# An attention-then-MLP kernel: loads of q and k, loads of v, turns and weight transposes put in another order, GpSimd's copies of v put later

## The chip, the cores and the metric

The kernel runs on one core of a Trainium2 chip. Its engines are TensorE (PE in the rows, its weight loads PEld), VectorE (DVE), ScalarE (ACT), GpSimd (POOL) and SyncE (SP). POOL and SP also issue DMAs, and each carries out its instructions in program order: an instruction that waits holds up everything behind it on the same engine. The metric is the device time of one execution in microseconds, lower is better.

## The reference

Two steps follow each other. The first is sliding-window causal attention over 8 batches, 8 heads, 576 rows, head size 64 and a window of 64:

```python
scores = scale * np.matmul(q, k.transpose(0, 1, 3, 2))
mask = (rel >= 0) & (rel < window)          # rel = row - column, window = 64
scores = np.where(mask, scores, -1e9)
attn = exp(scores - max); attn = attn / attn.sum()
x = attn @ v                                # heads side by side: x is 4608 x 512
```

The second is an MLP on the 4608 rows of x, with w_in 512 x 2048 and w_out 2048 x 512:

```python
h = x @ w_in
g = h * np.cos(h)
return g @ w_out
```

## The kernel before

The MLP is cut into nine **stages** `mt` of 512 rows (`MT`), called stage 0 to stage 8 here. A stage has two halves. In the first, 64 matmuls at L359 make h in 16 pieces `ff`; for each piece ScalarE takes the sine (L504), and VectorE multiplies (L507) and so frees the PSUM bank; five banks go round, so TensorE stops when VectorE stops. In the second half 64 matmuls at L519 multiply by w_out. Between two stages stand the 64 small matmuls of `values` (L338), which make the next stage's x from v and the attention weights; VectorE and ScalarE copy the result to `xT`.

The attention of the batches runs beside it. Batch b belongs to stage b-1: in that stage's second half TensorE makes the scores (L263), VectorE adds the mask (L286), ScalarE takes exp (L297), VectorE the reciprocal of the sum (L304), POOL multiplies to the weights `w` (L311, one instruction for a group of three or four blocks), and SP issues the DMA transpose of each group (`wT`, L323). A batch has ten such groups or so in two cuts (`CUTS`): those of the first cut are needed by the `values` at the end of the same stage, those of the second only a stage later.

What a batch needs before that comes in four steps:

- `load_chunk` (L146) loads q and k in five pieces each, with a cast from float32 to bf16; POOL issues them. `load_v` (L152) does the same for v, in five pieces.
- `turn` (L213) is a DMA transpose, issued by SP, from `q` to `qX` and from `k` to `kX`.
- `spread_q` (L221) is four VectorE copies from `qX` into `qB`, the form that the scores read.
- `spread_v` (L156) is two copies inside the tile of v which fill the rows that the `values` of odd blocks read; POOL makes them (L112, `v<-v`), or a DMA from SP (L160).

The order is a plan: `at(time, fn, ...)` puts a step at a planned time, in units where a stage is T = 32 and its second half begins at Q = 16, and `pump(time)` emits all steps that are due, between the matmuls. So the planned time sets where a step stands among the instructions of its engine, and nothing else; t0 = 32(b-1) is the start of batch b's stage. Before the change k and q of batch b are loaded in turns from t0 - T + 5.6, turned at the end of the stage before (t0 - 5.5), and spread at t0 + 6.2; v is loaded at t0 + 0.5 and spread at t0 + 14.45. Batch 2 has planned times of its own. A DMA of POOL also waits until the eighth DMA before it on POOL has landed, since eight semaphores go round.

Of the kernel before, what the change touches and what calls it, by code (L numbers as in the profile page):

```python
# [24 lines left out]
NC = 5  # L25
# [15 lines left out]
T = 2 * Q  # L41
# [17 lines left out]
def kernel(  # L59
# [326 lines left out]
    def at(time, fn, *args):  # L386
        plan.append((time, len(plan), fn, args))
# [25 lines left out]
    for b in range(1, B):  # L413
        t0 = T * (b - 1)
        if b == 1:
            for p in range(PAIRS):
                for lag, fn in ((0, tr_q), (0.01, tr_k), (0.02, put_q), (0.03, put_k)):
                    at(7 + 1.8 * p + lag, fn, b, p)
        else:
            for i, name in enumerate(("k", "q")):  # L420
                for c in range(NC):
                    at((4 + 0.5 * c + 2.5 * i if b == 2 else t0 - T + 5.6 + 1.8 * c + 0.9 * i), load_chunk, name, b, c)
                for c, (lo, hi) in enumerate(((0, 2), (2, 4), (4, 5))):
                    at(t0 - 5.5 + 1.8 * i + 0.6 * c, turn, name, b, lo, hi)
            for c, (lo, hi) in enumerate(((0, 4), (4, 5))):
                for h in range(2):
                    at(t0 + 6.2 + h + 2 * c, spread_q, b, h, lo, hi)
            for c in range(5):
                at(t0 + 0.5 + c, load_v, b, c)
            for half in range(2):  # L430
                at(t0 + (14.45 + 0.1 * half if b > 2 else 10), spread_v, b, half, "p" if b > 2 else "dma")
    for half in range(2):
        at(17.5, spread_v, 1, half, "dma")
    for p in range(PAIRS):
# [32 lines left out]
    turn, turn_h = iter(range(100)), iter(range(100))  # L467
# [17 lines left out]
    for mt in range(n_mt):  # L485
# [23 lines left out]
        half = n_ff // 2 if mt == 0 else n_ff  # L509
# [49 lines left out]
```

## Time and profile before

| | us |
|---|---|
| median of three runs (lowest, highest) | 363.88 (362.71, 371.75) |
| the profiled execution's own time | 364.2 |
| its span, first to last instruction | 362.4 |
| TensorE matmul busy | 304.8 (84%) |
| ScalarE busy | 235.9 (65%) |
| VectorE busy | 227.7 (63%) |
| GpSimd busy | 194.0 (54%) |
| mean granted TensorE clock | 0.939 |

The profiled execution took 364.2 us, 0.3 us over the median, of which 1.8 us lie outside the span. Stages begin, by their first matmul at L359, at 69.12 (stage 1), 100.73, 141.87, 184.19, 225.06, 265.90 and 302.79 us (stage 7). The share of busy time says little here, since the stages have waits in one place and none elsewhere; the rows further down are therefore cut by half stages.

### The profile page before, as it was taken

The page shows a single profiled execution, that of the slowest core. Times are in us where ns is not written, and L with a number is a line of the kernel's source. Part 1 is how long each engine was busy: PE and PEld are TensorE (multiplying, and loading weights), DVE is VectorE, ACT ScalarE, POOL GpSimd, SP SyncE. Part 2 cuts the span into 40 slices and gives each one's busy share as a digit, 9 for nine tenths or more (in the row PEclk, how much of TensorE's full clock was granted, in tenths as well). Part 3 has the DMA queues.
Part 4 walks back from the last instruction along what each step waited for, and adds up shares of the span by engine and source line. Part 5 has one row for each costly group of instructions (what it writes and reads, how often), then busy time and mean ns, then how long its engine had stood idle before and what let it go on. Part 6 is the DMA issues. An engine that isn't in the chain of part 4 may idle for free.

```text
span 362.4 us, 7495 instructions
## 1 busy us (share of the span) xinstructions
PE 304.8 (84%) x2413; PEld 152.9 (42%) x2452; DVE 227.7 (63%) x847; ACT 235.9 (65%) x785; POOL 194.0 (54%) x216
## 2 busy tenths in 40 slices
PE   4769959999993899919995599919996999999996
PEld 2544424444451355404552255404552455454443
DVE  5878836688671875539762786528764876832831
ACT  4887867768982499606983299707984699611720
POOL 9992375798698256870687446970673063000000
PEclk9999978999998699958999699988999899999999
DMA  7999992699999936999399947999399145212002
GB/s 97 180 210 208 178 165 32 116 161 246 114 131 166 189 39 108 128 197 105 81 114 144 218 50 95 149 177 128 75 117 204 49 71 90 90 40 78 1 31 87
DMA packets 166824, 44.02 MB, mean 121 GB/s; under 512 B 155520, under 2 KB 162304, under 8 KB 166784
## 3 DMA queue, kind: packets, MB, share of 16 engines
q0 software_dynamic: 99632, 18.36, 65.0%
q1 hardware_dynamic: 67008, 24.98, 37.4%
q8 instruction: 19, 0.31, 0.4%
q14 instruction: 21, 0.17, 0.2%
q10 hardware_dynamic: 144, 0.20, 0.2%
HBM read 36.70 MB, written 9.44 MB: 127 GB/s over the span
## 4 chain that ended last, share of the span: by engine, by line
PE 32%; DMA 27%; POOL 18%; issue 15%; DVE 5%; ACT 2%; SPq 0%; POOLq 0%; DVEq 0%
PE out_ps L519 17%; DMA qX<-q 14%; POOL w L311 10%; PE h_ps L359 10%; DMA v<-in_v_dram 5%; DMA w_out<-in_moe_w_out_dram 5%; POOL v L112 2%; DVE qB L221 2%; ACT e L297 2%; DMA q<-in_q_dram 2%; DVE gT L507 2%; PE o_ps L338 1%; POOL v L152 1%; PE s_ps L263 1%; DMA kX<-k 1%
## 5 line engine op out<-in xcount | busy, mean ns | idle before, releaser
L359 PE MATMUL h_ps<-xT,w_in 128*128 128x512 bf16 x557 | 136.0, 396 | 40.3 <-DVE gT L507 37.6
L504 ACT ACTIVATE sin<-h_ps 128x512 f32<-128x512 f32 x144 | 83.1, 598 | 83.2 <-DVE gT L507 42.7
L519 PE MATMUL out_ps<-w_out,gT 128*128 128x512 bf16 x543 | 132.0, 383 | 1.4 <-issue 0.7
L311 POOL TENSOR_TENSOR w<-e,rden 128x512 bf16<-128x512 f32 (+1 forms) x78 | 74.1, 957 | 82.1 <-issue 44.7
L507 DVE TENSOR_TENSOR gT<-h_ps,sin 128x512 bf16<-128x512 f32 x144 | 93.6, 686 | 29.5 <-ACT sin L504 29.1
L359 PEld LDWEIGHTS <-w_in 128*128 128x128 bf16 x576 | 57.4, 101 | 112.0 <-issue 52.6
L297 ACT ACTIVATE e<-s,negm 128x128 f32<-128x128 f32 x256 | 98.7, 388 | 4.8 <-DVE negm L286 4.8
L519 PEld LDWEIGHTS <-gT 128*128 128x128 bf16 x560 | 52.0, 99 | 50.7 <-issue 1.5
L286 DVE CUSTOM_DVE_ANT_0 s<-s_ps,mask 128x128 f32<-128x128 f32 x256 | 58.8, 286 | 2.6 <-PE s_ps L272 2.3
L297 ACT ACTIVATION_READ_ACCUMULATOR e<-s,negm 128x1 f32 x256 | 48.3, 189 | 0.0
L221 DVE COPY qB<-qX 64x2048 bf16<-64x2048 bf16 (+1 forms) x24 | 18.0, 751 | 40.6 <-DMA qX<-q 40.3
L152 POOL DMA_DIRECT2D v<-in_v_dram x40 | 34.1, 874 | 2.7 <-DMA k<-in_k_dram 2.0
L146 POOL DMA_DIRECT2D k<-in_k_dram x30 | 26.8, 894 | 13.8 <-PE h_ps L359 5.0
L146 POOL DMA_DIRECT2D q<-in_q_dram x30 | 26.8, 900 | 4.6 <-DMA q<-in_q_dram 4.3
L112 ACT COPY out_sb<-out_ps 128x512 f32<-128x512 f32 (+1 forms) x18 | 10.2, 566 | 27.0 <-PE out_ps L519 21.5
L304 DVE RECIPROCAL rden<-den 128x4 f32<-128x4 f32 (+1 forms) x80 | 13.9, 173 | 20.7 <-ACT e L297 19.1
L112 DVE CAST xT<-o_ps 128x512 bf16<-128x512 f32 x27 | 17.5, 679 | 11.3 <-PE o_ps L338 11.3
L263 PEld LDWEIGHTS <-qB 128*128 128x128 bf16 x216 | 17.3, 99 | 14.6 <-issue 0.8
L112 POOL COPY v<-v 64x2048 bf16<-64x2048 bf16 (+1 forms) x11 | 20.1, 1832 | 5.4 <-DMA v<-in_v_dram 5.1
L263 PE MATMUL s_ps<-kX,qB 128*128 128x128 bf16 x216 | 22.0, 220 | 0.0
L112 DVE COPY out_sb<-out_ps 128x512 f32<-128x512 f32 x18 | 12.4, 690 | 14.4 <-PE out_ps L519 14.4
L286 DVE DVE_READ_ACCUMULATOR2_ANT negm<- 128x1 f32 x256 | 21.3, 83 | 0.0
(53 smaller groups left out, 164.2 us busy)
## 6 DMA issues: line engine op xcount, KB each, us to landing
out_dram<-out_sb SPq DMA_DIRECT2D x16, 512.0 KB, 7.4
v<-in_v_dram POOLq DMA_DIRECT2D x32, 128.0 KB, 6.1
k<-in_k_dram POOLq DMA_DIRECT2D x24, 128.0 KB, 9.9
q<-in_q_dram POOLq DMA_DIRECT2D x24, 128.0 KB, 10.2
w_out<-in_moe_w_out_dram POOLq DMA_DIRECT2D x2, 1024.0 KB, 16.5
w_in<-in_moe_w_in_dram POOLq DMA_DIRECT2D x2, 768.0 KB, 11.8
wT<-w SPq DMA_TRANSPOSE x66, 2.5
out_dram<-out_sb SPq DMA_DIRECT2D x3, 256.0 KB, 2.0
```

The lines of the kernel that those rows point to most:

```text
L112: {"a": nc.scalar.copy, "p": nc.gpsimd.tensor_copy}.get(engine, nc.vector.tensor_copy)(out, in_)
L146: nc.gpsimd.dma_start(out=st[name, b][:n, c].rearrange("p (h d) -> p h d", h=H), in_=src.rearrange("h p d -> p h d"))
L152: nc.gpsimd.dma_start(out=vt.rearrange("p (h d) -> p h d", h=H), in_=v[b, :, c * 128:c * 128 + n, :].rearrange("h p d -> p h d"))
L221: nc.vector.tensor_copy(to.rearrange("d (m i) t -> d m i t", i=n), of[d, lo:hi, :, 0:64 * n].rearrange("d c a (i t) -> d (c a) i t", i=n))
L263: nc.tensor.matmul(out=s_ps[:, u].rearrange("p (a t) -> p a t", a=2), lhsT=q_block(b, p, j), rhs=k_blocks(b, p, j), start=True, stop=True, ...
L286: nc.vector.tensor_tensor_reduce(out=s[:, u], in0=s_ps[:, u], in1=mask[:, 2 - j % 2 if j else 0], scale=-scale if b else -1.0, scalar=BIG, ...
L297: nc.scalar.activation(e[:, u], s[:, u], AF.Exp, bias=negm[:, u:u + 1], scale=1.0 if n < n_first else -1.0, accum_out=den[:, u:u + 1])
L311: (nc.gpsimd if engine == "p" else nc.vector).tensor_tensor(out=w[:, 0:u], in0=e[:, 0:u], op=ALU.mult, in1=rden[:, 0:u].unsqueeze(2).to_br ...
L359: nc.tensor.matmul(out=st["h", ff], lhsT=w_in_sb[:, ks, ff * 128:ff * 128 + 128], rhs=st["xT", mt][:, ks], start=start, stop=stop)
L504: nc.scalar.activation(sin, h_ps, AF.Sin, bias=math.pi / 2.0)
L507: nc.vector.tensor_tensor(out=gt[:, e], in0=h_ps, in1=sin, op=ALU.mult)
L519: nc.tensor.matmul(out=o_ps[e], lhsT=gT[ff // 2][:, ff % 2, ms * 128:ms * 128 + 128], rhs=w_out_sb[:, ff], start=ff == 0, stop=ff == n_ff - 1)
```

## The change

The planned times of six kinds of steps change; no instruction's work changes but that a turn is cut in two pieces instead of three.

```diff
             for i, name in enumerate(("k", "q")):
                 for c in range(NC):
-                    at((4 + 0.5 * c + 2.5 * i if b == 2 else t0 - T + 5.6 + 1.8 * c + 0.9 * i), load_chunk, name, b, c)
-                for c, (lo, hi) in enumerate(((0, 2), (2, 4), (4, 5))):
-                    at(t0 - 5.5 + 1.8 * i + 0.6 * c, turn, name, b, lo, hi)
+                    at(t0 - T + 0.4 + 0.9 * (c + NC * i) if b > 2 else 4 + 0.5 * c if i else 27.5 + 0.9 * c, load_chunk, name, b, c)
+                for c, (lo, hi) in enumerate(((0, 4), (4, 5))):
+                    at((t0 + 3 if b == 2 and not i else t0 - T + 13.3 + 1.2 * i + (b == 2) * 9) + 0.6 * c, turn, name, b, lo, hi)
             for c, (lo, hi) in enumerate(((0, 4), (4, 5))):
                 for h in range(2):
-                    at(t0 + 6.2 + h + 2 * c, spread_q, b, h, lo, hi)
+                    at(t0 + 4.2 + h + 2 * c, spread_q, b, h, lo, hi)
             for c in range(5):
-                at(t0 + 0.5 + c, load_v, b, c)
+                at(t0 + 9.4 + 0.9 * c, load_v, b, c)
             for half in range(2):
-                at(t0 + (14.45 + 0.1 * half if b > 2 else 10), spread_v, b, half, "p" if b > 2 else "dma")
+                at(t0 + 24.2 + 0.1 * half, spread_v, b, half)
```

On SP, these are the rows from the second half of stage 5 to the start of stage 6 before the change. `wT<-w` are the transposes of batch 6's weights, `kX<-k` and `qX<-q` the turns of batch 7, `out_dram` the stores of stage 5.

```order
L323 DMA_TRANSPOSE wT<-w 128x4x128 x4
L323 DMA_TRANSPOSE wT<-w 128x3x128 x2
L323 DMA_TRANSPOSE wT<-w 128x4x128
L213 DMA_TRANSPOSE kX<-k 128x8x128 x2
L213 DMA_TRANSPOSE kX<-k 128x4x64
L323 DMA_TRANSPOSE wT<-w 128x3x128
L213 DMA_TRANSPOSE qX<-q 128x8x128
L323 DMA_TRANSPOSE wT<-w 128x3x128
L213 DMA_TRANSPOSE qX<-q 128x8x128
L213 DMA_TRANSPOSE qX<-q 128x4x64
L323 DMA_TRANSPOSE wT<-w 128x4x128
L382 DMA out_dram<-out_sb 128x2x512 x2
```

After the change SP's rows for the same stage 5 are these, from the stores of stage 4 on to those of stage 5; the turns are again batch 7's.

```order
L382 DMA out_dram<-out_sb 128x2x512 x2
L213 DMA_TRANSPOSE kX<-k 128x16x128
L213 DMA_TRANSPOSE kX<-k 128x4x64
L213 DMA_TRANSPOSE qX<-q 128x16x128
L213 DMA_TRANSPOSE qX<-q 128x4x64
L323 DMA_TRANSPOSE wT<-w 128x4x128 x4
L323 DMA_TRANSPOSE wT<-w 128x3x128 x2
L323 DMA_TRANSPOSE wT<-w 128x4x128
L323 DMA_TRANSPOSE wT<-w 128x3x128 x2
L323 DMA_TRANSPOSE wT<-w 128x4x128
L382 DMA out_dram<-out_sb 128x2x512 x2
```

The turns of batch 7 stood behind seven transposes of stage 5 and among the last three; now they stand ahead of all ten, and the spreads that read them stay in stage 6.

On POOL, stage 0 before the change has these rows after the loads of v for batch 1 (`v_78`); `k` and `q` are batch 2's, `w` batch 1's.

```order
L152 DMA v_78<-in_v_dram 64x8x64
L146 DMA k<-in_k_dram 128x8x64 x4
L146 DMA k<-in_k_dram 64x8x64
L146 DMA q<-in_q_dram 128x8x64 x4
L146 DMA q<-in_q_dram 64x8x64
L311 TENSOR_TENSOR w<-e,rden 128x512 x2
L311 TENSOR_TENSOR w<-e,rden 128x384 x8
L311 TENSOR_TENSOR w<-e,rden 128x512 x2
```

After the change the same place on POOL reads so.

```order
L152 DMA v_78<-in_v_dram 64x8x64
L146 DMA q<-in_q_dram 128x8x64 x4
L146 DMA q<-in_q_dram 64x8x64
L311 TENSOR_TENSOR w<-e,rden 128x512 x2
L311 TENSOR_TENSOR w<-e,rden 128x384 x7
L146 DMA k<-in_k_dram 128x8x64
L311 TENSOR_TENSOR w<-e,rden 128x384
L146 DMA k<-in_k_dram 128x8x64 x2
L311 TENSOR_TENSOR w<-e,rden 128x512
L146 DMA k<-in_k_dram 128x8x64
L311 TENSOR_TENSOR w<-e,rden 128x512
L146 DMA k<-in_k_dram 64x8x64
```

The five loads of k moved from ahead of the first `w` to behind the ninth and later ones.

On POOL in stage 1 before the change, the last loads and clears are followed by batch 2's groups and then by the loads of the next stage; batch 2's v was spread by SP.

```order
L146 DMA k<-in_k_dram 64x8x64
L146 DMA q<-in_q_dram 64x8x64
L367 MEMSET qB_76 128x1152
L311 TENSOR_TENSOR w<-e,rden 128x512 x6
L311 TENSOR_TENSOR w<-e,rden 128x384 x4
L152 DMA v_78<-in_v_dram 128x8x64 x4
```

After the change the loads that stand last there are those of v (`v_77`), and the copies of v stand between the fifth and the sixth group.

```order
L152 DMA v_77<-in_v_dram 128x8x64 x2
L152 DMA v_77<-in_v_dram 64x8x64
L367 MEMSET qB_76 128x1152
L311 TENSOR_TENSOR w<-e,rden 128x512 x5
L112 COPY v_77<-v_77 64x3x512
L112 COPY v_77<-v_77 64x4x512
L311 TENSOR_TENSOR w<-e,rden 128x512
L311 TENSOR_TENSOR w<-e,rden 128x384 x4
L146 DMA k<-in_k_dram 128x8x64 x4
```

The first cut of batch 2 has six groups, so one group of it now stands behind the copies. In stage 2 the copies stand behind the sixth group of a first cut of six, and from stage 3 on behind the fifth group, where the first cut has four.

## Rows read from the trace of the kernel before

**Rows 1.** Waits: engine line waited for, us in total, times, longest us.

```profile
DVE qB L221 <- DMA qX<-q: 40.3, 6, 9.4
...
PE h_ps L359 <- DVE gT L507: 37.6, 11, 8.8
```

**Rows 2.** Windows by half stage: length; busy us per engine; PEclk, DMA share, GB/s.

```profile
69.12:83.75 14.63, 13.61 (x69) 6.13 (x65) 11.62 (x20) 9.36 (x16) 14.63 (x17) 1.00 1.57 177
...
100.73:124.65 23.92, 16.55 (x64) 6.93 (x67) 14.16 (x22) 10.38 (x17) 17.13 (x18) 0.79 1.78 172
...
141.87:167.21 25.34, 15.70 (x65) 6.75 (x67) 13.70 (x21) 10.12 (x17) 17.35 (x18) 0.80 1.70 166
...
184.19:208.07 23.88, 15.70 (x65) 6.68 (x68) 12.79 (x21) 10.37 (x17) 17.33 (x18) 0.86 1.74 173
208.07:225.06 16.99, 16.86 (x164) 9.20 (x163) 12.69 (x89) 16.92 (x78) 8.46 (x9) 1.00 0.49 69
225.06:248.91 23.85, 15.51 (x65) 6.77 (x67) 12.97 (x22) 10.36 (x17) 16.96 (x18) 0.86 1.78 174
...
265.90:285.81 19.91, 15.64 (x65) 6.70 (x67) 13.09 (x22) 10.37 (x17) 8.60 (x8) 0.91 1.18 156
...
302.79:316.70 13.91, 13.80 (x63) 6.36 (x65) 10.59 (x18) 10.38 (x17) 1.04 (x1) 1.00 0.40 95
```

**Rows 3.** Timeline of stage 4: start, us, instruction, idle before and its releaser.

```profile
201.47 0.81 DVE L221 COPY qB<-qX 64x2048 bf16<-64x2048 bf16 x1 [8.84 <-DMA qX<-q]
...
202.90 1.67 DVE L221 COPY qB<-qX 64x2048 bf16<-64x2048 bf16 x1
202.92 1.01 PE L359 MATMUL h_ps<-xT,w_in 128*128 128x512 bf16 x2 [7.34 <-DVE gT L507]
```

**Rows 4.** Windows, a stretch of stage 0.

```profile
47.50:51.30 3.80, 0.03 (x1) 0.00 (x0) 0.00 (x0) 2.02 (x12) 3.80 (x6) 0.82 1.83 190
```

**Rows 5.** Timelines of stage 0: POOL's loads, TensorE's next instruction.

```profile
45.97 4.22 POOL L146 DMA_DIRECT2D q<-in_q_dram  x5
...
51.31 0.61 PE L320 MATMUL tw_ps<-ident,w 128*128 128x128 bf16 x4 [3.78 <-POOL w L311]
```

**Rows 6.** Groups of POOL by form: count, busy us, mean ns, idle before.

```profile
L311 POOL TENSOR_TENSOR w<-e,rden 128x512 bf16<-128x512 f32 x46 | 48.0, 1047 | 57.0 <-issue 36.1 <-DVE rden L304 20.7
...
L311 POOL TENSOR_TENSOR w<-e,rden 128x384 bf16<-128x384 f32 x32 | 26.2, 826 | 25.1 <-DVE rden L304 15.0 <-issue 8.6 <-DMA wT<-w 0.8
```

**Rows 7.** Timelines of stage 1: POOL's last clear and groups, TensorE's values.

```profile
85.66 1.13 POOL L367 MEMSET qB<- 128x1152 bf16 x1
87.81 1.03 POOL L311 TENSOR_TENSOR w<-e,rden 128x512 bf16<-128x512 f32 x1 [1.02 <-DVE rden L304]
...
95.98 1.04 POOL L311 TENSOR_TENSOR w<-e,rden 128x512 bf16<-128x512 f32 x1 [0.98 <-DVE rden L304]
...
99.51 1.20 PE L338 MATMUL o_ps<-wT,v 128*64 128x64 bf16 x64
```

**Rows 8.** Timeline of POOL in stage 4: first loads, last load of k, copies.

```profile
185.29 4.26 POOL L152 DMA_DIRECT2D v<-in_v_dram  x5
...
198.00 0.69 POOL L146 DMA_DIRECT2D k<-in_k_dram  x1
...
200.24 3.79 POOL L112 COPY v<-v 64x1536 bf16<-64x1536 bf16 x2
```

**Rows 9.** DMA issues from 185 to 200 us: count, KB each, median us to landing.

```profile
q<-in_q_dram POOLq DMA_DIRECT2D x4, 128.0 KB, 11.9
...
k<-in_k_dram POOLq DMA_DIRECT2D x1, 64.0 KB, 12.1
...
wT<-w SPq DMA_TRANSPOSE x3, 7.5
```

**Rows 10.** DMA issues from 213 to 222.5 us.

```profile
wT<-w SPq DMA_TRANSPOSE x7, 2.4
```

**Rows 11.** Timeline of POOL in stage 1, a load beside VectorE's spread copies.

```profile
78.10 1.32 POOL L146 DMA_DIRECT2D q<-in_q_dram  x1
```

## The prediction

> **What bounds the kernel now.** I read the waits first. VectorE waited 40.3 us in six pieces at the spread (L221) for `qX` to land, and TensorE 37.6 us for VectorE's multiply [rows 1]. The two are one wait, as stage 4 shows: the spread stands idle 8.84 us until `qX` lands at 201.47, and the next matmul of h starts at 202.92 after 7.34 us of idling for `gT` [rows 3]. VectorE runs in order, so the multiplies behind the spread free no PSUM bank.
>
> Then the half stages. Stage 7 has no attention work, and its first half takes 13.91 us with TensorE busy for 13.80. The first halves of stages 1 to 6 take 14.63, 23.92, 25.34, 23.88, 23.85 and 19.91 us for the same 64 matmuls [rows 2]. That is more than the wait alone: the granted clock of the five long halves is 0.79 to 0.91 on the mean, that of stages 1 and 7 is 1.00 [rows 2], so after TensorE has stood idle it runs at the lower of its two levels for a while. The second half of stage 4 takes 16.99 us with TensorE busy for 16.86, so it is bound by TensorE itself [rows 2]. A stage without waits is thus 13.9 + 17.0 = 30.9 us. There is one more hole: from 47.5 to 51.3 us, in stage 0, TensorE does nothing [rows 4]. It waits 3.78 us for POOL's first `w`, and POOL is issuing the five loads of q from 45.97 to 50.19 [rows 5].
>
> **The change, part by part.**
>
> *Turns a stage half earlier.* They move ahead of a stage's weight transposes, and some 14 planned units earlier, while the spread comes only 2 units earlier. `qX` then lands in the stage before the one that spreads it, half a stage ahead of need, so the wait at L221 should go in every stage. The gain is each first half's excess over 13.91: 0.7 + 10.0 + 11.4 + 10.0 + 9.9 + 6.0 = **48.1 us**. It includes the lower clock, as the hole that causes it is gone, and spread copies that took 1.67 us beside POOL's copies of v [rows 3] but no longer meet them. The four spread copies themselves cost TensorE nothing: VectorE is busy 10.59 us of stage 7's first half [rows 2], which leaves over 3 us. Two pieces instead of three save SP an issue; a larger piece is not in the trace. Its landing is bounded by a smaller piece's and twice that, and neither end matters with half a stage in hand, so it counts as 0.
>
> *Loads of batch 2's k behind `w` in stage 0.* Five loads leave the place ahead of POOL's first `w`; five like them took 4.22 us [rows 5]. TensorE's hole is 3.8 us, so the gain is **3.8 us**. The clock that would come back behind it I leave out.
>
> *Stage 1 pays for that.* The five loads of k now fall among the later `w` of stage 0 and the start of stage 1. POOL's loads and clears end at 86.79 today and the first `w` is asked for at 87.81 [rows 7]. The first would move to 86.79 - 3.8 + 4.2 = 87.2, or to 83.0 if all five loads fall into gaps; the second moves to 87.81 - 3.8 - 0.7 = 83.3. I take 87, since the gaps lie between groups that POOL was already late with. Five groups at 1.05 us [rows 6] end at 92.2. Behind them now stand the copies of v, 3.79 us [rows 8], and they wait for loads that are issued last, until about 84 us, and land some 9 us later (12 us at the end of a long row of loads [rows 9]): 93. So the copies end near 96.8, the sixth group, which the `values` of stage 2 need, near 97.9, and its transpose adds the 2.5 us that lie today between 97.02 and the `values` at 99.51 [rows 7]: 100.4. Without this, the `values` would start at 99.51 - 4.5 = 95.0. TensorE waits **5.4 us** more. From below: loads in gaps and v landed in time, 83.3 + 5.2 + 3.8 + 1.05 + 2.5 = 95.9, so 1 us. From above, with v landing 12 us after issue, 8.5 us.
>
> *POOL's loop in stages 2 to 5.* Call L the time at which POOL issues a stage's first load, 1.1 us after the stage begins (185.29 against 184.19). Today the copies of v have their v early, since v is loaded first; now v is last. The last but one of the 15 loads of stage 4 is issued at 198.00 and lands 12.1 us later [rows 8, 9], that is L + 24.8; I take 24.5 for the last v that the copies need. The copies end at L + 28.3. Behind them stand five groups, 3 x 0.83 + 2 x 1.05 = 4.6 us [rows 6], and then the next loads: 32.9 us round, against 30.9 for TensorE. `values` are wanted 29.7 us after the stage begins (99.51 - 69.12 - 0.7), that is at L + 28.6 while L lags by 1.1. POOL lags 0.8 us more after stage 2 and 1.5 us more after stage 3; the `values` then wait 0.4, 1.9 and 1.9 us at the ends of stages 3, 4 and 5: **4.2 us**. Stage 6 loads v alone and has room. If v lands at L + 23 there is no wait; at L + 26.5 it is about 11 us. The load phase itself is covered: it takes 15 us in stage 4 (185.29 to 200.24), a load beside spread copies takes 1.32 us instead of 0.85 [rows 5, 8, 11], so 1 us a stage for two, and the first `w` is asked for some 17 us after L [rows 7].
>
> *The sum.* 364.2 - 48.1 - 3.8 + 5.4 + 4.2 = 321.9. Against the median of the runs the profiled execution is 0.3 us high, so I say **322 us**.
>
> **The rivals.**
>
> *All of it hides.* The loads of v land at L + 23 and the k loads of stage 0 fall into gaps: 364.2 - 48.1 - 3.8 + 1 = 313, or 315 with the stage 1 wait halved. For it: transposes in front of the loads are fewer than today. Against it: TensorE's stage of 30.9 leaves POOL 2 us too little by the measured landings.
>
> *The weight transposes are late.* On SP they now stand behind the turn of q, which waits for the tenth load. Beside loads a weight transpose lands after 7.5 us, without them after 2.4 [rows 9, 10], so the queues slow each other. The tenth load is issued near L + 8 and lands 12 us later [rows 9]: L + 20. Two turns and four transposes at about 1.3 us of issue end at L + 28, and the fourth lands at L + 30.5 to L + 33. The `values` start there and not at L + 28.6, the next L comes some 2.3 us behind that, and the round is 33 to 35.5 us; at 34, 4 x 3.1 = 12.4 us instead of 4.2: 330. The Trainium skill, DMA: Bandwidth & Descriptors, section Issuing engines are not separate DMA queues, speaks for this case: DMAs from SP and GpSimd end up on the same 16 engines and interleave, so an early turn takes time from the loads of v. The landings of 7.5 and 2.4 us agree with it.
>
> *No gain.* The wait moves whole from `qX` to v: the copies hold POOL's later groups and the next loads. That needs a round as long as today's stage, 40.8 us from 184.19 to 225.06, so v must land at L + 40.8 - 8.4 = L + 32.4; beyond it the change loses. With L + 35 the round is 43.4 us, and 364.2 + 4 x 2.6 + 5.4 - 3.8 - 0.7 - 6.0 = 370. Against it stands that all 15 loads land by L + 25 today with as many transposes and stores beside them. The DMA share of 0.49 in stage 4's second half against 1.74 in the first [rows 2] says there is room.
>
> *It doesn't do what it says.* VectorE still waits for `qX`, because SP reaches the turn late, behind the stores and the loads of q. `qX` would have to land 20 us after it is due. With half the waits left: 364.2 - 24 - 3.8 + 5.4 + 4.2 = 346.
>
> **How the numbers follow.** The forecast, 317 to 328, has 0.45; all hidden, 312 to 317, 0.24; late weight transposes, 328 to 338, 0.21; half the waits left, 340 to 356, 0.03; no gain, 0.06; below 312, 0.01. The range of 313 to 336 leaves out about a tenth above and less below. A measurement of this kernel tells about 2% (7.3 us) from no change. So faster takes all cases but the fourth's slower end and the no-gain case: 0.93, same 0.04, slower 0.03.
>
> **What would show it.** In the profile after, the wait of VectorE for `qX` is gone or under 3 us, and the first halves of stages 2 to 6 take 14 to 15 us at a clock near 1.00. TensorE has no hole at 47.5 us. At the end of stage 1 the `values` (L338) wait about 5 us, for POOL's `w` or its copies of v, and there are waits of some 2 us at the ends of stages 3 to 5. POOL waits for v before its copies. If instead L338 waits for `wT`, the second rival is right; if it waits for nothing, the first. The forecast is wrong if the wait at L221 stays, or if stages stay near 40 us with POOL's loop as the releaser.

## The result, and the profile after

The changed kernel takes 333.25 us (median of four runs, 332.31 to 333.94) against 365.18 us of the kernel before on the same chip: 0.9145 of the time, 95% interval 0.9078 to 0.9212. One of the four runs before, of 371.75 us, fell in a slower state and is left out of that ratio. The forecast was 322, its range 313 to 336. The profiled execution took 332.9 us, its span is 331.2 us, the mean granted clock 0.968 (0.939 before).

The waits come first again: engine and line, what it waited for, us in total, times, longest us.

```profile
DVE xT L112 <- PE o_ps L338: 26.5, 15, 4.4
...
PEld L338 <- issue: 19.8, 19, 3.5
PE o_ps L338 <- DMA wT<-w: 14.8, 8, 3.4
...
POOL v L112 <- DMA v<-in_v_dram: 3.6, 2, 2.4
```

VectorE's 40.3 us for `qX` and TensorE's 37.6 us for `gT` [rows 1] are gone from the list. In their place TensorE waits 14.8 us at the `values` (L338) for `wT`, the transposes of the attention weights, and its weight loads stand idle there too. POOL waits for v, but only 3.6 us.

The windows by half stage have the columns of [rows 2]: the first halves of stages 1, 2, 3 and 4, then the second half of stage 4, the `values` at its end, and the first half of stage 5.

```profile
68.12:82.98 14.86, 14.86 (x67) 6.48 (x65) 11.65 (x19) 8.64 (x15) 14.86 (x17) 0.90 2.06 189
...
103.65:120.04 16.39, 16.39 (x70) 7.05 (x68) 11.69 (x21) 8.74 (x15) 11.30 (x13) 0.85 2.01 173
...
138.54:152.52 13.98, 13.98 (x72) 6.44 (x68) 11.90 (x21) 8.87 (x16) 10.89 (x13) 1.00 1.57 179
170.66:184.65 13.99, 13.99 (x72) 6.45 (x68) 11.30 (x20) 9.26 (x16) 13.30 (x15) 1.00 1.54 152
184.65:200.40 15.75, 15.75 (x100) 8.00 (x98) 11.76 (x85) 15.69 (x73) 9.20 (x9) 1.00 1.75 160
200.40:207.67 7.27, 2.04 (x65) 1.67 (x64) 1.18 (x3) 3.07 (x7) 7.19 (x9) 0.76 0.75 91
207.67:223.26 15.59, 15.59 (x70) 6.84 (x68) 11.70 (x21) 8.63 (x15) 10.59 (x13) 0.89 1.71 179
```

In every one of these first halves TensorE is busy throughout. Those of stages 3 and 4 take 14.0 us where they took 25.3 and 23.9 [rows 2]; those of stages 1, 2 and 5 take 14.9, 16.4 and 15.6 us at a mean clock of 0.90, 0.85 and 0.89, and each stands right behind a wait at L338. The 7.27 us from 200.40 to 207.67 hold 64 matmuls that take 1.20 us where nothing holds them [rows 7].

TensorE's timeline at that place shows the waits one by one.

```profile
200.40 0.35 PE L338 MATMUL o_ps<-wT,v 128*64 128x64 bf16 x10
201.76 0.44 PE L338 MATMUL o_ps<-wT,v 128*64 128x64 bf16 x16 [1.01 <-DMA wT<-w]
203.06 0.44 PE L338 MATMUL o_ps<-wT,v 128*64 128x64 bf16 x16 [0.86 <-DMA wT<-w]
206.86 0.88 PE L338 MATMUL o_ps<-wT,v 128*64 128x64 bf16 x22 [3.36 <-DMA wT<-w]
```

SP's timeline of stage 4 shows where `wT` was held: start, us that SP spent on issuing, then the instruction.

```profile
182.30 7.11 SPq L213 DMA_TRANSPOSE kX<-k  x2
192.73 6.44 SPq L213 DMA_TRANSPOSE qX<-q  x2
199.26 7.00 SPq L323 DMA_TRANSPOSE wT<-w  x5
```

POOL made the first group of the stage at 188.70 to 189.74, as its timeline has it below, yet SP issues the first `wT` only at 199.26. In between SP stands 3.3 us, nearly all of it until the q that the turn needs has landed, and the two pieces of that turn occupy it from 192.73 to 199.17.

```profile
172.16 4.26 POOL L146 DMA_DIRECT2D k<-in_k_dram  x5
...
188.70 1.04 POOL L311 TENSOR_TENSOR w<-e,rden 128x512 bf16<-128x512 f32 x1 [0.42 <-DVE rden L304]
...
197.70 3.41 POOL L112 COPY v<-v 64x1536 bf16<-64x1536 bf16 x2 [2.40 <-DMA v<-in_v_dram]
201.19 4.39 POOL L311 TENSOR_TENSOR w<-e,rden 128x384 bf16<-128x384 f32 x5
205.52 0.94 POOL L146 DMA_DIRECT2D k<-in_k_dram  x1
```

The same happens in stage 0, at the `values` that end it (here in two portions of 32 matmuls, 0.7 us each in the kernel before):

```profile
62.58 0.32 PE L338 MATMUL o_ps<-wT,v 128*64 128x64 bf16 x8 [2.29 <-DMA wT<-w]
...
67.60 0.58 PE L338 MATMUL o_ps<-wT,v 128*64 128x64 bf16 x14 [2.52 <-DMA wT<-w]
```

Stage by stage, from the starts of the stages (before: as told under the table of times; after: 68.12, 103.65, 138.54, 170.66, 207.67, 240.24 and 271.20 us), beside what the prediction's terms say for each:

| stage | before | after | difference | predicted | missed by |
|---|---|---|---|---|---|
| 0 and what is ahead of it | 69.12 | 68.12 | -1.0 | -3.8 | +2.8 |
| 1 | 31.61 | 35.53 | +3.9 | -0.7 + 5.4 | -0.8 |
| 2 | 41.14 | 34.89 | -6.3 | -10.0 | +3.7 |
| 3 | 42.32 | 32.12 | -10.2 | -11.4 + 0.4 | +0.8 |
| 4 | 40.87 | 37.01 | -3.9 | -10.0 + 1.9 | +4.2 |
| 5 | 40.84 | 32.57 | -8.3 | -9.9 + 1.9 | -0.3 |
| 6 | 36.89 | 30.96 | -5.9 | -6.0 | 0 |
| 7 and 8 | 59.6 | 60.0 | +0.4 | 0 | +0.4 |

Most of the gain of the first halves came as forecast. The 11 us missing against 322 lie at the ends of stages 0, 2, 3 and 4, where `wT` is late, and in the lower clock of the first halves of stages 2 and 5. The end of stage 1 waits for `wT` too, but a wait of that size was in the forecast.

### The profile page after: what moved, and what is told of

It is laid out like the page before. It is cut to its first block, busy times and chain, and to the rows that moved or that the text cites. A ratio compares the mean times of both kernels' runs of the same rounds, so it can differ in the third digit from the quotient of the medians.

```text
span 331.2 us, 7510 instructions
## 1 busy us (share of the span) xinstructions
PE 304.9 (92%) x2452; PEld 154.2 (47%) x2452; DVE 222.0 (67%) x847; ACT 236.0 (71%) x785; POOL 197.2 (60%) x218
## 4 chain that ended last, share of the span: by engine, by line
PE 53%; DMA 18%; POOL 11%; DVE 7%; issue 5%; ACT 3%; SPq 2%; POOLq 0%; DVEq 0%
PE h_ps L359 27%; PE out_ps L519 19%; DMA q<-in_q_dram 7%; DMA wT<-w 6%; POOL w L311 4%; DMA v<-in_v_dram 3%; POOL k L146 3%; DVE gT L507 3%; POOL v L112 2%; SPq L213 2%; ACT e L297 2%; PE o_ps L338 2%; PE s_ps L272 1%; DMA k<-in_k_dram 1%; PE s_ps L263 1%
## 5 line engine op out<-in xcount | busy, mean ns | idle before, releaser
L359 PE MATMUL h_ps<-xT,w_in 128*128 128x512 bf16 x576 | 133.3, 392 | 0.8 <-ACT xT L112 0.6
L152 POOL DMA_DIRECT2D v<-in_v_dram x40 | 35.1, 888 | 15.3 <-PE h_ps L359 5.2
L112 ACT COPY out_sb<-out_ps 128x512 f32<-128x512 f32 (+1 forms) x18 | 10.2, 566 | 28.1 <-PE out_ps L519 22.6
L338 PE MATMUL o_ps<-wT,v 128*64 128x64 bf16 x576 | 15.1, 204 | 15.1 <-DMA wT<-w 14.8
L304 DVE RECIPROCAL rden<-den 128x4 f32<-128x4 f32 (+1 forms) x80 | 13.9, 173 | 21.2 <-ACT e L297 20.3
L146 POOL DMA_DIRECT2D k<-in_k_dram x30 | 25.7, 872 | 0.0
L112 POOL COPY v<-v 64x2048 bf16<-64x2048 bf16 (+1 forms) x13 | 22.4, 1720 | 4.0 <-DMA v<-in_v_dram 3.6
L338 PEld LDWEIGHTS <-v 128*64 128x64 bf16 x576 | 12.4, 118 | 20.5 <-issue 19.8
L286 DVE DVE_READ_ACCUMULATOR2_ANT negm<- 128x1 f32 x256 | 21.2, 83 | 0.0
## 6 DMA issues: line engine op xcount, KB each, us to landing
v<-in_v_dram POOLq DMA_DIRECT2D x32, 128.0 KB, 11.4
```

What stands on the lines that cost most here:

```text
L112: {"a": nc.scalar.copy, "p": nc.gpsimd.tensor_copy}.get(engine, nc.vector.tensor_copy)(out, in_)
L146: nc.gpsimd.dma_start(out=st[name, b][:n, c].rearrange("p (h d) -> p h d", h=H), in_=src.rearrange("h p d -> p h d"))
L152: nc.gpsimd.dma_start(out=vt.rearrange("p (h d) -> p h d", h=H), in_=v[b, :, c * 128:c * 128 + n, :].rearrange("h p d -> p h d"))
L286: nc.vector.tensor_tensor_reduce(out=s[:, u], in0=s_ps[:, u], in1=mask[:, 2 - j % 2 if j else 0], scale=-scale if b else -1.0, scalar=BIG, ...
L338: nc.tensor.matmul(out=o_ps[64 * h:64 * h + 64, 64 * i:64 * i + 64], lhsT=vtiles[b % 2][:, max(j - 1, 0), 128 * p + 64 * h:128 * p + 64 * ...
L359: nc.tensor.matmul(out=st["h", ff], lhsT=w_in_sb[:, ks, ff * 128:ff * 128 + 128], rhs=st["xT", mt][:, ks], start=start, stop=stop)
```

## The experiments

**The theory** from this profile: the turn of q now stands on SP ahead of the first cut's `wT`; SP waits there for the last loads of q, and beside the loads of v the pieces take it several us each, so `wT` leaves late (the prediction's second rival, in this kernel's numbers). **The rivals:** POOL's loop through the late v (the prediction's own fourth term), the size of the pieces, and DMA engines so full that a transpose is late wherever it stands.

| kernel | us | of before [95%] | L338 waits for `wT` | L221 waits for `qX` |
|---|---|---|---|---|
| the change | 333.25 | 0.9145 [0.9078, 0.9212] | 14.8 | not listed |
| old turns, new loads | 377.53 | 1.0368 [1.0314, 1.0423] | 5.2 | 57.7 |
| new turns alone | 345.47 | 0.9478 [0.9396, 0.956] | 12.3 | 0.9 |
| three pieces | 331.12 | 0.9088 [0.9028, 0.9149] | 10.4 | not listed |
| k ahead in stage 0 | 336.28 | 0.9189 [0.9105, 0.9273] | 13.0 | not listed |
| turns behind the first cut | 338.55 | 0.9305 [0.9251, 0.9359] | 6.0 | 19.8 |
| v first | 334.82 | 0.9185 [0.9114, 0.9255] | 12.6 | not listed |
| no loads of v | 322.25 | 0.8832 [0.8749, 0.8914] | 7.8 | not listed |
| turns in gaps | 319.47 | 0.876 [0.8705, 0.8815] | 3.3 | not listed |
| the same, copies behind the sixth group | 319.35 | 0.8757 [0.8693, 0.8821] | 2.4 | not listed |
| the same, v first in stage 1 | 318.23 | 0.8722 [0.8662, 0.8783] | 1.3 | not listed |

**The turns back at their old place, loads as changed.**

```diff
-at((t0 + 3 if b == 2 and not i else t0 - T + 13.3 + 1.2 * i + (b == 2) * 9) + 0.6 * c, turn, name, b, lo, hi)
+at(t0 - 5.5 + 1.8 * i + 0.6 * c if b > 2 else t0 + 3 + 0.4 * c if not i else t0 - T + 23.5 + 0.4 * c, turn, name, b, lo, hi)
```

in three pieces as before (the line with the cuts is not shown). Expected:

> The changed kernel with the turns of batches 3 to 7 at their old planned times and in their old three pieces, at the end of the stage among its last weight transposes; loads of q and k first, v later, copies late, as in the changed kernel. It tells what the order of the loads does without the turns. If the wait for qX came from the turns meeting the loads of the next stage, whichever they are, the wait at L221 comes back with 5 to 8 us a stage and none at L338: 345 to 358 us. If it came from v standing first among the loads, the wait stays away: 318 to 328 us.

Measured: 377.53 us, slower than before the change. The wait at L221 is back, as the first case had it, but at 11.5 us a stage instead of 5 to 8, so the time lies far above its 345 to 358. The waits:

```profile
DVE qB L221 <- DMA qX<-q: 57.7, 5, 13.5
PE h_ps L359 <- DVE gT L507: 49.6, 5, 11.9
```

The rest of the change without the turns is a loss. The turns at the end of a stage meet the next stage's loads, as they did in the kernel before, and the spreads that read them now stand 2 units earlier. What took the wait at L221 away is the place of the turns.

**The turns alone, in the kernel before.**

```diff
-for c, (lo, hi) in enumerate(((0, 2), (2, 4), (4, 5))):
-    at(t0 - 5.5 + 1.8 * i + 0.6 * c, turn, name, b, lo, hi)
+for c, (lo, hi) in enumerate(((0, 4), (4, 5)) if b > 2 else ((0, 2), (2, 4), (4, 5))):
+    at(t0 - T + 13.3 + 1.2 * i + 0.6 * c if b > 2 else t0 - 5.5 + 1.8 * i + 0.6 * c, turn, name, b, lo, hi)
```

> The kernel before with one part of the change alone: the turns of batches 3 and later at t0 - T + 13.3 and in two pieces; loads, spreads and copies of v stay as before. If the place of the turns ahead of the weight transposes is what takes away the wait at L221 and what makes the weight transposes late, the wait at L221 is gone from stage 2 on, L338 waits for wT for 15 us or more (the q loads end later here, as they alternate with k behind v), and the time is 328 to 350 us. If the new load order is what removes the wait at L221, it stays at some 30 us in all and the time is 355 to 368 us.

Measured: 345.47 us. L221 waits 0.9 us in all, and `wT` is late instead.

```profile
DVE qB L221 <- DMA qX<-q: 0.9, 1, 0.9
...
PE o_ps L338 <- DMA wT<-w: 12.3, 9, 2.2
```

This is the first case of the two on the time and on L221; the wait for `wT` is somewhat smaller than it asked (12.3 for 15 or more). Earlier turns give about 20 us by themselves. The other 12 us to the changed kernel come with the loads, spreads and copies, of which only k's place in stage 0 and v's place with its copies were undone by themselves below, each by less than the intervals tell.

**Three pieces of a turn instead of two**, cuts (0, 2), (2, 4), (4, 5) at 0.4 units apart.

> The changed kernel with the turns cut in three pieces (8, 8 and 4 blocks) as before the change, at the same planned times. If a piece of 16 blocks holds SP for longer than the data needs (it took up to 7.4 us on SP, a piece of 8 blocks at most 3.4 us), the weight transposes come some 3 us earlier in four stages and the time is 322 to 328 us. If SP is held because the queue takes no more until data has moved, three pieces are held as long in sum: 331 to 336 us.

Measured: 331.12 us, 0.9088 of before, with intervals that overlap the change's. This is the second case. L338 waits 10.4 us for `wT`, not 14.8, and 2.0 us more for the copies of v. In stage 4 the three pieces hold SP for 7.73 us, no less than the two held it:

```profile
185.56 7.73 SPq L213 DMA_TRANSPOSE qX<-q  x3
```

Whether the pieces' size matters by 2 us stays open; it isn't what makes `wT` late.

**The loads of batch 2's k ahead of `w` in stage 0, as before.**

```diff
-27.5 + 0.9 * c, load_chunk
+4 + 0.5 * c + 2.5 * i, load_chunk
```

> The changed kernel with batch 2's loads of k put back ahead of the first w of stage 0, as before the change; everything else is the changed kernel's. It measures that part alone. By the prediction's term TensorE's hole of 3.8 us in stage 0 comes back, and the k loads no longer fall between stage 0's late groups. Theory 1 (what is late at the end of stage 0 are weight transposes behind the turn of q, 5.3 us of waiting at L338): the hole takes the place of that waiting, POOL is free 4 us earlier in stage 1, and the time is 331 to 335 us, the same. If the part was worth its 3.8 us: 336 to 338 us.

Measured: 336.28 us, interval overlapping the change's. The hole of stage 0 is back, in TensorE's timeline:

```profile
46.69 1.90 PE L519 MATMUL out_ps<-w_out,gT 128*128 128x512 bf16 x8
51.55 0.45 PE L320 MATMUL tw_ps<-ident,w 128*128 128x128 bf16 x4 [2.96 <-POOL w L311]
```

and stage 1 begins at 71.37 us, not 68.12. The `values` of that stage start 5.6 us later (65.36 for 59.72), but then wait 2.6 us for `wT` instead of 4.8, so some 3 us of the step are left at the end of stage 0. The medians differ by 3 us as well, which is the second case; but the runs lie from 331.79 to 336.85 and the intervals overlap, so on the whole time it is not shown.

**All turns of batches 3 and later behind the first cut's `wT`.**

```diff
-t0 - T + 13.3 + 1.2 * i + (b == 2) * 9
+t0 - T + ((26.3 if b < 5 else 23.2) if b > 2 else 22.3) + 1.2 * i
```

> The changed kernel with one edit: the turns of batches 3 to 7 get planned times of t0 - T + 26.3 (batches 3 and 4) or t0 - T + 23.2 (batches 5 to 7), so that on SP they stand behind the weight transposes that the next values need, and not ahead of all ten. Loads, spreads and POOL's order are those of the changed kernel. Theory 1, the weight transposes are late because SP reaches them only after the turn of q: the values (L338) no longer wait for wT (14.8 us in the changed kernel), the lower clock behind those waits (about 4 us in the first halves of stages 2 and 5) goes too, the wait for qX stays away, and the time is 317 to 322 us. Theory 2, the 16 DMA engines are full in that stretch and the order on SP only decides who is late: the wait moves to qX at L221 or stays at L338, and the time is 330 us or more. Theory 3, POOL's copies of v bind: L338 waits as long as before but for POOL, 328 us or more.

Measured: 338.55 us, with the wait moved to `qX`, which by the words above is the second theory's result. By stages it is mixed. Stages 4 and 5 take 31.0 us each, with L338 at its 1.20 us, as the first theory has it. In stages 2 and 3 the first halves take 23.0 and 27.2 us, because the wait at L221 is back. Which of the two theories holds is left to the run with the turns in gaps. SP's timeline where it ends its work of stage 2, and VectorE's, both in TensorE's stage 3, which begins at 141.8 us:

```profile
147.50 7.69 SPq L213 DMA_TRANSPOSE qX<-q  x2
...
160.55 0.68 DVE L221 COPY qB<-qX 64x2048 bf16<-64x2048 bf16 x1 [12.07 <-DMA qX<-q]
```

With a first cut of six groups, "behind the first cut" is so late that the turn runs into the next loads, which POOL issues from 143.45 us on; it lands at 160.5, 13 us after its issue. A turn has a window: behind the last load of q and the first cut's `wT`, ahead of the next stage's loads.

**v loaded first again, and copied ahead of the groups.**

```diff
-at(t0 + 9.4 + 0.9 * c, load_v, b, c)
+at(t0 + 0.25 + 0.02 * c, load_v, b, c)
-at(t0 + 24.2 + 0.1 * half, spread_v, b, half)
+at(t0 + 14.45 + 0.1 * half, spread_v, b, half)
```

> The changed kernel with one part undone: the loads of v go first in a stage again (t0 + 0.25) and POOL copies v at t0 + 14.45, ahead of the groups; the turns stay where the change put them, so the loads of q and k end five loads later. If the turn of q, which stands ahead of the weight transposes on SP and waits for the last load of q, is what makes the values late, it is later still by some 4 us a stage: L338 waits 25 us or more in all for wT and the time is 340 to 352 us. If POOL's copies of v behind late loads are what the stages lose, L338's wait falls under 8 us and the time is 322 to 328 us.

Measured: 334.82 us, which neither expected. L338 waits 12.6 us for `wT`. SP's timeline of stages 3 and 4:

```profile
158.96 3.67 SPq L213 DMA_TRANSPOSE qX<-q  x2
162.73 13.87 SPq L323 DMA_TRANSPOSE wT<-w  x10
...
195.90 3.63 SPq L213 DMA_TRANSPOSE qX<-q  x2
199.62 3.83 SPq L323 DMA_TRANSPOSE wT<-w  x3
```

The stages begin at 139.47 and 174.19 us, so the turn of q starts 19.5 and 21.7 us into them, no later than the 22.1 us of stage 4 after the change. And with no loads of v behind q its two pieces take SP 3.6 us, not 6.4. The order of v and q thus trades one delay for another, and my 4 us a stage for q loaded later was wrong. That the time is the same with POOL's copies out of the loop speaks against that loop as the bound.

**No loads of v from batch 3 on**, all else as changed.

```diff
-for c in range(5):
+for c in range(5 if b < 3 else 0):
```

> The changed kernel without the loads of v for batches 3 and later (that part of the computation is left out: those values are made from what is left in the tile); SP's order, the loads of k and q and the copies stay. If the weight transposes are late because SP stands at the turn of q until the last load of q has landed, SP's wait there stays (the loads of q are issued at the same time) and L338 still waits 8 us or more: 326 to 333 us. If they are late because the loads of v run beside the turn of q and hold its issue (3 to 7 us a piece on SP), pieces of the turn take under 2.5 us on SP, L338 waits under 4 us from stage 2 on, and the time is 316 to 323 us.

Measured: 322.25 us, 11 us less: the second case, though the waiting for q that the first case names is there too. SP's timeline of stage 4, which begins at 166.39 us:

```profile
187.63 3.64 SPq L213 DMA_TRANSPOSE qX<-q  x2
191.37 14.44 SPq L323 DMA_TRANSPOSE wT<-w  x10
```

The turn of q still starts 21.2 us into the stage, for 22.1: that part is the waiting for q. But it takes 3.64 us of SP, for 6.44, and the first `wT` leaves at 25.0 instead of 28.6. L338 takes 1.92 us at that stage's end, for 7.34, and 1.20 to 1.92 from the end of stage 2 on. Nearly all of the 7.8 us of waits that are left lie at the ends of stages 0 and 1, to which the edit doesn't reach. So of the 3.6 us by which the first `wT` of stage 4 leaves earlier, 2.8 are the price of issuing a turn beside the loads of v. The edit also frees POOL's copies from waiting for v; that this is not what gave the gain is argued from the releaser, which after the change was `wT`, and from the run before.

**The turns in the gaps.** In stages 1 and 2 the turn of k stays ahead and that of q goes behind the fifth or sixth `wT`; from batch 5 on both stand behind the first cut's four; batch 2's turn of q goes ahead of the first `wT` of stage 0.

```diff
-at((t0 + 3 if b == 2 and not i else t0 - T + 13.3 + 1.2 * i + (b == 2) * 9) + 0.6 * c, turn, name, b, lo, hi)
+at((((21.5, t0 + 3), (24.4, 13.3), (24.4, 13.3))[b - 2][name == "k"] + (b > 2) * (t0 - T) if b < 5 else t0 - T + 23.2 + 0.7 * i) + 0.3 * c, turn, name, b, lo, hi)
```

> The changed kernel with the turns put where SP neither waits for loads of the same stage nor meets the loads of the next one: in stages 1 and 2 the turn of k stays at t0 - T + 13.3 and the turn of q moves behind the weight transposes of the first cut (t0 - T + 24.4); from batch 5 on both stand behind the four transposes of the first cut (23.2 and 23.9); batch 2's turn of q stands ahead of the first weight transpose of stage 0. If the order on SP is all that makes the weight transposes late, L338 waits for wT for under 5 us in all, every stage from 1 on takes about 31 us (33 for stage 1, where POOL's copies of v stand ahead of the sixth group), the wait at L221 stays under 2 us, and the time is 315 to 321 us. If the 16 DMA engines are so full that transposes are late wherever they stand, L338 or L221 waits 10 us or more and the time is 328 to 336 us. If the theory that POOL's round trip for v bounds the stages is right, the stages stay at 33 us each with POOL's copies of v as the releaser: 325 to 330 us.

Measured: 319.47 us, 0.876 of before, better than both kernels, and the first case but for stages 1 and 2 (38.7 and 32.7 us). Stages 2 to 6 end with L338 at 1.20 us, stages 3 to 6 take 30.95 us each, the `values` at the end of stage 0 take 0.69 and 0.70 us, and stage 1 begins at 62.89 us. No load was left out, and the DMA share of the first halves of stages 4 and 5 is 1.67 and 1.84 (1.54 and 1.71 after the change), so full DMA engines are not the reason; the order on SP is. What is left is stage 1, in TensorE's timeline:

```profile
93.95 0.32 PE L338 MATMUL o_ps<-wT,v 128*64 128x64 bf16 x8
96.85 0.76 PE L338 MATMUL o_ps<-wT,v 128*64 128x64 bf16 x36 [2.58 <-POOL v L112]
100.92 0.75 PE L338 MATMUL o_ps<-wT,v 128*64 128x64 bf16 x20 [3.31 <-DMA wT<-w]
```

Here the prediction's third term is seen bare: POOL's copies wait 3.94 us for v until 93.39, the sixth group comes behind them, and its `wT` behind that.

**Stage 1: the copies of v behind the sixth group** (`spread_v` of batch 2 at t0 + 25.9).

> The kernel with the turns in gaps, with one more step moved: POOL's copies of v for batch 2 stand behind the sixth group of the first cut instead of ahead of it, so the loads of v still come last in stage 1. If the wait left at the end of stage 1 is POOL's, as the prediction said (the copies wait for v until about 93.4 and the sixth group waits behind them), the values no longer wait for the sixth transpose but for the copies alone, which end near 96.9: the 7.7 us of L338 there fall to 3.5 to 4.5, released by POOL's v, and the time is 315 to 317.5 us. If the sixth transpose is late for a reason of SP's (behind the turn of q), L338 keeps 6 us or more and the time is 318 to 320 us.

Measured: 319.35 us; L338 takes 6.59 us there, not 3.5 to 4.5.

```profile
96.81 0.94 PE L338 MATMUL o_ps<-wT,v 128*64 128x64 bf16 x36 [2.19 <-POOL v L112]
100.14 0.75 PE L338 MATMUL o_ps<-wT,v 128*64 128x64 bf16 x20 [2.39 <-DMA wT<-w]
```

Both cases were half right. The first wait is for the copies at 96.8, as expected; but the sixth `wT`, whose group was now ready at 91.8, still left SP only at 96.83, because in that place the turn of q stands ahead of it (92.43 to 96.73).

**Stage 1: v loaded first as well** (`load_v` of batch 2 at t0 + 0.25, batch 3's turn of q at 25.9).

> The same, and the loads of v for batch 2 go first in stage 1, ahead of batch 3's k and q, whose turn of q moves behind all six transposes of the first cut. v lands some 18 us earlier, so if late v is what is left at the end of stage 1, the copies end with the sixth group's end plus 3.4 us, L338 there waits under 1.5 us, stage 2's first half returns to 14.0 us at full clock, and the time is 311 to 314 us. If the later loads of k and q (five loads, some 4 us) make the turn of k or the transposes behind it late, L338 waits 3 us or more at the end of stage 1, or VectorE waits for qX in stage 2, and the time is 316 us or more.

Measured: 318.23 us, not told apart from the last two by their intervals. L338 takes 2.67 us there and stage 2's first half 13.99. But v now delays k, and TensorE's scores wait in the middle of stage 1:

```profile
79.61 0.61 PE L263 MATMUL s_ps<-kX,qB 128*128 128x128 bf16 x4 [2.38 <-DMA kX<-k]
```

Stage 1 takes 36.6 us. In none of the orders tried did its fifteen loads and what came from stage 0 fit without a wait somewhere; moving the wait from v to k takes 2 us off stage 1 and 1 us off the whole time, which the intervals do not tell from nothing.

## Why the prediction was off by 11 us, step by step

The time lies inside the range, and the median of the forecast was missed because another of the written cases came true: late weight transposes, 328 to 338. That the range holds the result is owed to that case being in it, not to the sum.

*The turns.* Right: the wait at L221 is gone, and the first halves without a wait ahead of them take 14.0 us at a clock of 1.00. The two runs with one half of the change each show that it is the turns' place and not the loads'. What the prediction put as 48.1 us came except where a new wait brought the lower clock back: 14.86, 16.39 and 15.59 us in stages 1, 2 and 5, against 13.99 in stage 4, that is 0.9, 2.4 and 1.6 us of the miss.

*Stage 0.* The hole is gone, but only 1.0 us came, since the step was costed by POOL alone. On SP batch 2's turn of q was moved too, behind the first of the stage's `wT`. It pushed the next ones in among the loads of k, beside which three of them took 4.1 us in the median to land (58.4 to 62.2 us). The `values` waited 2.3 and 2.5 us and took 5.3 us over their undisturbed time. With that turn put ahead, stage 1 begins at 62.89 us, so the term was 6.2 us, not 3.8. The difference is the clock that the prediction left out. The stretch behind the hole in the kernel before, and the same work after the change, in the columns of [rows 2]:

```profile
51.31:62.98 11.67, 11.18 (x93) 5.90 (x95) 6.73 (x48) 7.33 (x36) 5.81 (x7) 0.77 0.95 62
47.49:56.65 9.16, 9.16 (x96) 4.91 (x94) 6.64 (x49) 9.16 (x48) 5.92 (x7) 1.00 0.54 87
```

The first has a mean clock of 0.77 and takes 2.5 us more.

*Stage 1 pays.* About right in size: 5.4 predicted; 3.8 us at L338 in the changed kernel (4.99 - 1.20) and 6.5 in the one with the turns in gaps (7.71 - 1.20). But the size was luck: the chain is another. The copies were to wait for v until 93. In the changed kernel they found their v landed, and took 3.41 us for 3.79 [rows 8]; what came late was the end of the five groups, at 94.2 and not at the 92.2 of the sum, since each of them waited for VectorE:

```profile
93.19 1.04 POOL L311 TENSOR_TENSOR w<-e,rden 128x512 bf16<-128x512 f32 x1 [0.50 <-DVE rden L304]
94.17 3.41 POOL L112 COPY v<-v 64x1536 bf16<-64x1536 bf16 x2
```

In the kernel with the turns in gaps the groups came earlier, and the wait for v is there as forecast.

*POOL's loop.* Its numbers held in stage 4 and its conclusion did not. The copies were released 25.5 us after the first load (predicted 24.5), and the next loads came 33.4 us after it (predicted 32.9). But the `values` stood for `wT` until 206.86, long after the copies' end at 201.1. With the turns out of the way, the copies start 23.8 us after the first load in stage 4, with a wait of 0.65 us for v, and 22.4 us after it in stage 5, without any; both stages take 30.95 us. So v's lateness was itself in part a result of the turns beside it: the term of 4.2 us should have been near 0 once `wT` is in time.

*The term that was missing* is the second rival, which had 0.21 and gave 330. Its chain is what happened: the turn of q waits for the last q, and the transposes behind it are late. It put the first `wT` of a stage at about 23 us after the first load (20 and two turns at 1.3); in stage 4 it was 27.1 (199.26 - 172.16). Most of the difference is SP's time for the two pieces: 6.4 us where the prediction had 2.6. The large piece was costed at 0 because its landing has half a stage in hand. That is true of its landing and not of its issue, which holds all that stands behind it on SP.

*What is not settled.* At the ends of stages 1 to 5 L338 took 3.8, 1.6, 1.2, 6.1 and 0.1 us over its 1.20 after the change, but 1.7, 5.6, 0, 4.4 and 0 with k ahead in stage 0, and 4.2, 0.7, 0.5, 3.7 and 1.9 with three pieces. What decides at which stage it falls was not tried. The third `wT` of stage 4, issued at 201.88, landed only at 206.81, when the two ahead of it took 2.5 us each. No load ran beside it; two packets of the kind that the profile calls instruction did, as the last section tells. By the landings of the two ahead, 2.5 us of that stage's 6.1 would be theirs (an estimate); no run was made without them.

*Where the account stops.* That the order on SP makes `wT` late is shown by the runs that changed that order, the turns in gaps above all. That the loads of v lengthen a turn's issue is shown by leaving them out. How the two share the 11 us was not measured.

## What to carry to other kernels

When a transfer is moved on an in-order issuing engine, cost two things apart: when it lands, and how long it stands at the head of the queue, waiting for its input and issuing beside other traffic. Look up who stands behind it; here a turn with half a stage in hand held transposes that had none. And give each transfer a window from both sides: ahead of the scarce transposes it blocks them, behind them it runs into the next stage's loads.

## What the runs showed of the hardware

Issuing a DMA transpose can take much longer beside loads. The view of line L213 after the change gives count, then ns as least, median and most.

```profile
L213 SPq DMA_TRANSPOSE qX<-q x12: 1199/2497/6320, 55.0 to 229.6; - x12
L213 SPq DMA_TRANSPOSE kX<-k x12: 1205/2780/7394, 70.2 to 222.7; - x12
```

A piece, large or small, holds SP for 1.2 us at the least and for 6.3 or 7.4 us at the most, and in stage 4 the turn of q held it 6.44 us with loads of v beside it and 3.64 without. The Trainium skill, DMA: Bandwidth & Descriptors, section Issuing engines are not separate DMA queues, says that the time a sequencer takes to start a DMA is usually small beside the DMA itself. Here it isn't: the first piece of q in stage 4 was 5.1 us on SP (from 192.73) and landed 7.4 us after its start. The other statement of that section, that DMAs of SP and GpSimd share 16 engines and interleave, is in line with the packets from 190.5 to 199.3 us, when loads (q0) and transposes (q1) moved in the same stretch; that they used the same engines the rows do not show:

```profile
q0 software_dynamic: 5611, 0.70, 124.8%
q1 hardware_dynamic: 3384, 0.85, 60.3%
```

Second, a wait of TensorE costs more than its length. The granted clock, which has the levels 1.2 and 2.4 GHz, was 0.76 of the upper one on the mean in the 7.27 us of waits at the end of stage 4 and 0.89 in the half stage behind, which took 1.6 us more than one at the upper level throughout (15.59 for 13.99).

Third, a transpose can be late with no load beside it. From 201.9 to 206.8 us after the change, the time in which the third `wT` of stage 4 was under way, the profile has these packets on other queues, of 16 and 8 KB, at 204.90 and 203.70 us:

```profile
q8 instruction: 1, 0.02, 1.2%
q14 instruction: 1, 0.01, 0.4%
```

Over the traces of all twelve kernels, the transposes `wT<-w` with neither a load nor such a packet beside them, 181 of them, landed 2.3 to 2.6 us after their issue. The 233 with such a packet and no load took 2.3 to 5.0, with medians of 2.7 to 3.3 us by kernel. That goes together in every trace; no run took the packets away, so the cause is not shown.
